# Weight sums kept in DRAM, and the sums of the seventh group's third block moved, in a routing-attention and squared-ReLU kernel

## The chip, the cores and the metric

The kernel runs on one core of a Trainium2 chip. The metric is the device time of one execution in microseconds (us). The median of three runs stands for a kernel, and a profiled execution of its own shows where the time goes. The page and the traces name the engines: PE is TensorE (PEld its weight loads), DVE is VectorE, ACT is ScalarE, POOL is GpSimd, and SP is SyncE, which here issues most of the DMAs.

## The reference, cut to what matters

```python
batch, n_heads, seq, head_dim = (4, 8, 768, 64); n_clusters = 16
n_tokens, d_model, d_ff = (3072, 512, 2048)
# attention, per batch and head: queries see only keys of their own cluster
mask = q_assign[:, :, :, None] == k_assign[:, :, None, :]
scores = np.where(mask, scale * q @ k.T, -1e9)
attn_out = softmax(scores) @ v
# its rows are the tokens of the second part
x = attn_out.transpose(0, 2, 1, 3).reshape(3072, 512)
h = x @ w_in                 # "up":   512 -> 2048
g = np.maximum(h, 0.0) ** 2
out = g @ w_out              # "down": 2048 -> 512
```

## The kernel before, in words

The attention comes first: 16 pairs of heads (`for p in range(NG)`), up to about 319 us. After it each of the four batches (`for n, b in enumerate(FEED)`) runs an up product with the squared ReLU into `g`, and a down product from `g` into the output. All instructions around the change are put out by hand, in program order on each engine (`manual_schedule`). Each engine, and SP with its DMAs, works through its own list in that order, and an instruction that waits holds up what is behind it on its list.

**Products by Strassen's scheme.** Both products save multiplications: a 2 x 2 block product is made by seven block products of sums of blocks. For the up product the sums of the weights are made by `w_sums(i)` for a group `i` of 0 to 7 (`F2` is 8): four operations on POOL fill one tile `w_s` of 128 x 1024 numbers (512 KB). There are two such tiles (tags `s1` and `s2`), used in turn. `w_sums` is called 8 times in every batch with the same weights, so 32 times. In batch 0 its first two calls stand at the ends of the last two attention pairs, and the others in `first_up`, one at the end of each group. In batches 1 to 3 the calls stand in `up`, one group ahead of use. In the down product the same two tags hold the second-level sums of a unit (`l`).

**Batch 0.** `first_up` runs eight groups. Each makes seven products into PSUM (`banks`: six buffers); ScalarE copies product 1 (L756), and VectorE adds the others into `g` (L750) in the order 6, 2, 7, 5, 4, 3 (`combine`). Between these additions `Rounding` brings the rest of the weights to their rounded form. It works on blocks of 512 columns: blocks 0 to 15 are `w_in`, 16 to 31 are `w_out`. A block is loaded by SP (L122, `load_ahead`), goes through two operations of ScalarE (L133, L139), three of VectorE (L145, L149, L153) and one of POOL (L161). `prepare(i)` stands behind the copy of group `i`: at `i = 0` it holds blocks 16 to 20, all on ScalarE and ahead of the copy of group 1. `behind` adds up the last pair's sums (L494) behind group 0. `first_down` is the down product of batch 0.

**Batches 1 to 3.** `up` runs the eight groups; a part of the products (all groups but the last two) has a second level of sums, whose weight sums also come from POOL (L839). When a group's results are squared, VectorE makes two kinds of sums of it for the down product: `first_level(g, f)` for the first two of the three column blocks, and `third_sums(g, n, f)` for the third block. The latter are four operations into a tile `third`, which a DMA stores in `g_far` (L1109); the blocks of `g` that are wanted as they are go there by `store_third` (L1096). For group 6 `third_sums` stands at the end of `up`, and its store is put out later by `Down.run` on ScalarE's queue; for group 7 it stands in `Down.run` behind the first unit.

`Down.run` goes through *units*, 14 in batches 1 and 3 and 7 in batch 2. A unit is seven products of four matmuls each (L1113), 6.26 us of TensorE. `parts` makes the sums of the next unit; `x[0][1] - s[:, 1]` (L1282, in the traces the helper's line L551) makes the operand of a unit's last product; `load_right` (L1072) brings the right-hand operands of the next unit, and `load_left` (L1151) those of the third block. `stage.parts` is passed to `up` as `behind_seven`, so that the first unit's sums are made inside `up`.

The traces give operations of small helpers the line of the helper: `sub` is L551, `plus` is L990, `matmul` of the up product L793.

Of the kernel before, what the change touches and what calls it, by code (L numbers as in the profile page):

```python
# [8 lines left out]
F32 = mybir.dt.float32  # L9
# [9 lines left out]
P = 128  # L19
# [6 lines left out]
def kernel(  # L26
# [10 lines left out]
    nc = tc.nc  # L37

    B, H, S, D = q.shape
# [19 lines left out]
    sp = ctx.enter_context(tc.tile_pool(name="sp", bufs=1))  # L59
    dram = ctx.enter_context(tc.tile_pool(name="dram", bufs=3, space=bass.MemoryType.DRAM))  # L60
    dram_x = ctx.enter_context(tc.tile_pool(name="dram_x", bufs=1, space=bass.MemoryType.DRAM))
# [135 lines left out]
    odd = const.tile([P, 2], F32, name="odd")  # L197
# [350 lines left out]
    H2, F2, M2 = KT // 2, FT // 2, DM // 2  # L548

    def sub(out, a, b, eng=nc.vector):  # L550
        return eng.tensor_tensor(out=out, in0=a, in1=b, op=ALU.subtract)  # L551
# [11 lines left out]
        sub(t4, t2, x[1][0])  # L563
        yield x, t1, t2, x[0][1], t4

    def w_sums(i, odd=0):
        lo, hi = slice(i * P, (i + 1) * P), slice((F2 + i) * P, (F2 + i + 1) * P)
        a = [[w_in[:, H2 * g2 : H2 * (g2 + 1), cols] for g2 in range(2)] for cols in (lo, hi)]
        w_s = sp.tile([P, 4, H2, P], F32, name="w_s", tag=f"s{(i + odd) % 2 + 1}")
        s1, s2, s3, s4 = (w_s[:, j] for j in range(4))  # L570
        nc.gpsimd.tensor_tensor(out=s1, in0=a[1][0], in1=a[1][1], op=ALU.add)  # L571
        sub(s2, s1, a[0][0], nc.gpsimd)
        sub(s3, a[0][0], a[1][0], nc.gpsimd)
        sub(s4, a[0][1], s2, nc.gpsimd)
        return a, s1, s2, s3, s4

    def tile_of(pair, i):
# [148 lines left out]
    def bank_tile(width):  # L726
        return banks.tile([P, width], F32, name="bank", tag="bank")
# [159 lines left out]
        plus(middle, c34, middle)  # L887
        yield

    def up(b, g, n, x, behind_seven, stores):  # L890
        flat = g.rearrange("p f h n -> p (f h n)")
        odd = n == B - 1
        w_next = w_sums(0, odd)
        lefts, rights, done = {}, {}, []
        for i in range(F2):
            w, w_next = w_next, w_sums(i + 1, odd) if i + 1 < F2 else None
            ((c11, c12), (c21, c22)), product = group(i, g, w, x)
            ends, late = i >= F2 - 2, i % 2

            def result(j):  # L900
                bank = bank_tile(TB)
                product(j, bank)
                return bank

            def add(j, *results):
                bank = result(j)
                for out, to in results:
                    plus(out, bank, to)

            def levels_1():  # L910
                if done:
                    first_level(g, done[0])

            def levels_2():
                if done:
                    third_sums(g, n, done.pop(0))()

            def two():
                add(2, (c11, c11))
                square(c11)  # L920
                if i < F2 - 1:
                    levels_2()

            if i < 2:
                nc.scalar.copy(out=c11, in_=result(1))
            elif not late:
                next(unit_1)
                if ends:
                    load_right(1)
            if not (late or ends):  # L930
                lefts[4] = second_lefts(4, i)
            add(6, (c12, c11))
            if i < F2 - 1:
                levels_1()
            if i == 1:
                rights[1] = second_rights(1, x[0][0][0])
            if not late or ends:
                two()
            if i == 0:
                rights[4] = second_rights(4, x[4])  # L940
            add(7, (c21, c12))
            if ends:
                levels_1()
            if i == F2 - 1:
                behind_seven()
            r = spare_tile.rearrange("p i n -> p (i n)")
            if late and not ends:
                unit_4 = second(lefts.pop(4), rights[4], r, 0, TB)
                next(unit_4)
            add(5, (c22, c21), (c12, c12))  # L950
            square(c22)
            if i == F2 - 2:
                levels_2()
            if ends:
                sub(c21, c21, result(4))
            elif late:
                next(unit_4)
                unit_1 = second(
                    second_lefts(1, i + 1), rights[1], flat, 2 * TB * (i + 1), 2 * TB
                )  # L960
                next(unit_1)
                both = g[:, F2 + i - 1 : F2 + i + 1, 0]
                sub(both, both, r.rearrange("p (i n) -> p i n", i=2))
                for k in range(2):
                    square(both[:, k])
                two()
            add(3, (c12, c12))
            if ends:
                square(c21)
            (square if i < F2 - 1 else square_by_dve)(c12)  # L970
            if i == F2 - 1:
                stores.append(third_sums(g, n, i - 1))
            done.extend([i] if ends else [i - 1, i] if late else [])
        xT.pop(b)

# [13 lines left out]
    def plus(out, one, two):  # L989
        nc.vector.tensor_tensor(out=out, in0=one, in1=two, op=ALU.add)  # L990
# [50 lines left out]
    g_far = [dram_x.tile([F2, P, 7, P], F32, name=f"g_far{n}") for n in range(B)]  # L1041
# [53 lines left out]
    def store_third(g, n, f, queue=nc.sync):  # L1095
        queue.dma_start(g_far[n][f, :, 1:3], g[:, F2 + f, :, THIRD])  # L1096
        if n % 2 == 0:
            queue.dma_start(g_far[n][f, :, 0], g[:, f, 0, THIRD])

    def third_sums(g, n, f):  # L1100
        if f < F2 - 1:
            store_third(g, n, f)
        a = block_of(g, f, THIRD)
        third = outp.tile([P, DM], F32, name="third", tag="osb").rearrange("p (j n) -> p j n", j=4)
        plus(third[:, 0], a[1][0], a[1][1])
        sub(third[:, 1], third[:, 0], a[0][0])
        sub(third[:, 2], a[0][0], a[1][0])
        sub(third[:, 3], a[0][1], third[:, 1])
        return lambda queue=nc.sync: queue.dma_start(g_far[n][f, :, 3:7], third)  # L1109

    def times(bank, left, rhs):
        for f in range(F4):
# [8 lines left out]

    class Down:
        def __init__(self, b, g, n):
            self.up_stores = []
            self.b, self.g, self.n = b, g, n
            both = n % 2
            self.units = (
                [(0, 1), (0, 4), (1, 4), (1, 1)] if both else [(0, 1), (0, 4)]
            ) + [(of, j) for j in RIGHT_ORDER[2:] for of in range(1 + both)]
            a = blocks(g, TWO)  # L1130
            s1, s2 = (s_home(i) for i in range(2))
            self.lefts = {
                1: a[0][0], 2: a[0][1], 3: s1, 4: a[1][1], 5: s1, 6: s2, 7: a[1][0]
            }
            self.a, self.s1, self.s2 = a, s1, s2
            self.count = 0
            self.stores = []
# [111 lines left out]
        def store(self, queue=nc.scalar):  # L1249
            for of, to in self.stores:  # L1250
                for i in range(2):
                    self.store_block(of, to, i, queue)
            self.stores = []

        def run(self):
            first_level(self.g, F2 - 1)
            waiting = None
            for u, (of, j) in enumerate(self.units):
                x, s = self.ahead
# [9 lines left out]
                times(one[:, 0], x[0][0], y[0][0])  # L1269
                nc.scalar.copy(out=copied, in_=one[:, 0])  # L1270
                if u == 0:
                    store_third(self.g, self.n, F2 - 1, nc.scalar)
                    self.up_stores.pop()(nc.scalar)
                self.store()
                times(two[:, 0], x[0][1], y[1][0])
                times(two[:, 1], s[:, 1], slot(1))
# [15 lines left out]
                        sub(self.s1, self.a[0][1], self.s2)  # L1292
                    self.parts()
                if u == 0:
                    store = third_sums(self.g, self.n, F2 - 1)
                    self.find_results()
                    if self.n % 2:
                        self.load_left(4)
                        self.load_left(1)
                    store()  # L1300
                if waiting:
                    next(waiting, None)
                waiting = self.combine(of, j, one, two, five, copied, last)
# [91 lines left out]
    x_summed = {}  # L1395
# [8 lines left out]
    for n, b in enumerate(FEED):  # L1404
        g = gp.tile([P, FT, 2, TB], F32, name="g")
        if n == 0:
            first_up(b, g, Rounding())
            first_down(b, g)
            again = nc.values_load(flag[0:1, 0:1], min_val=0, max_val=1)
            with tc.issue_after(last_w_sum[0]):  # L1410
                sum_x(1, 4)
            manual.enter_context(
                tc.manual_schedule(engines={E.PE, E.DVE, E.Activation, E.Pool, E.SP})
            )
            more = fast.enter_context(
                tc.tile_pool(name="more", bufs=2, space=PSUM, reuse_waits="tile")
            )
        else:
            stage = Down(b, g, n)
            up(b, g, n, x_summed.pop(n)[-1], stage.parts, stage.up_stores)  # L1420
            stage.run()
    manual.close()
    fast.close()
# [190 lines left out]
```

## Time and profile before

| what | value |
|---|---|
| median of 3 runs | 881.0 us (880.43 to 881.81) |
| the profiled execution | 880.63 us, of which span 878.8 us |
| TensorE busy | 870.7 us, granted clock 0.999 |
| VectorE busy | 755.9 us |
| ScalarE busy | 385.9 us |
| POOL busy | 182.4 us |
| DMA | 136.05 MB, mean 155 GB/s |

The stages of the span, from the trace:

| stage | us | TensorE busy | VectorE busy | POOL busy |
|---|---|---|---|---|
| attention | 0 to 319.4 | 317.8 | 274.0 | 24.7 |
| batch 0, up | 319.4 to 393.1 | 73.7 | 70.2 | 47.7 |
| batch 0, down | 393.1 to 441.8 | 48.7 | 43.6 | 3.2 |
| batch 1, up | 441.8 to 512.2 | 70.4 | 59.4 | 30.8 |
| batch 1, down | 512.2 to 599.8 | 87.6 | 71.7 | 5.4 |
| batch 2, up | 599.8 to 670.2 | 70.4 | 61.7 | 31.8 |
| batch 2, down | 670.2 to 714.1 | 43.9 | 38.8 | 5.3 |
| batch 3, up | 714.1 to 784.4 | 70.3 | 64.1 | 33.6 |
| batch 3, down, and the end | 784.4 to 878.8 | 87.9 | 72.3 | 0.0 |

How to read it: the span goes from the first instruction to the last, and the time of the execution is a little longer. TensorE's busy time counts a matmul from its start to a modelled end; consecutive matmuls overlap, so a mean duration in the page (0.486 us for 128 x 384) is longer than the distance at which such matmuls follow each other (9.03 us for 28 of them, so 0.3225 us). An f32 product of one tile shows as two matmul records. A wait is listed with the engine that ended it. In a timeline a line gives the start, the length, the engine, the line of the program, the operation with its output and inputs, how many instructions are merged, and in brackets the idle time ahead of it and what ended it.

### The profile page before, as it was taken

How to read it: one execution, taken by the hardware profiler on the slowest of the kernel's cores; microseconds unless marked ns; L12 is line 12 of the kernel's file. 1: busy time of each engine (PE TensorE's matmuls, PEld its weight loads, DVE VectorE, ACT ScalarE, POOL GpSimd, SP SyncE). 2: the span in 40 equal slices, each digit the busy share in tenths (PEclk: the TensorE clock that was granted, in tenths of full speed). 3: DMA queues.
4: the chain of work that ended last, by engine and by line, in shares of the span. 5: the costliest groups of instructions: out<-in, count | busy, mean ns of one | idle time of the engine just before them, and what ended most of it. 6: DMA issues, size and time to landing. Idle time of an engine off the chain costs nothing.

```text
span 878.8 us, 14998 instructions
## 1 busy us (share of the span) xinstructions
PE 870.7 (99%) x5487; PEld 597.9 (68%) x5487; DVE 755.9 (86%) x1359; ACT 385.9 (44%) x621; POOL 182.4 (21%) x240
## 2 busy tenths in 40 slices
PE   9999999999999999999999999999999999999997
PEld 5444444444444455568866689997767977769997
DVE  6799888888888999999859986797899898997786
ACT  5877667777765657750034420002543015440000
POOL 0000010000000236740055300005540064500000
PEclk9999999999999999999999999999999999999999
DMA  7777786866764235226701347681024730147563
GB/s 253 175 188 202 214 267 177 209 181 194 203 168 124 83 139 172 89 95 227 277 25 43 101 145 217 186 258 37 31 91 148 240 116 25 37 134 230 166 203 124
DMA packets 166402, 136.05 MB, mean 155 GB/s; under 512 B 58826, under 2 KB 140082, under 8 KB 166066
## 3 DMA queue, kind: packets, MB, share of 16 engines
q1 hardware_dynamic: 148546, 118.67, 45.7%
q10 hardware_dynamic: 17776, 16.36, 5.9%
q8 instruction: 45, 0.74, 0.3%
q14 instruction: 35, 0.29, 0.1%
HBM read 82.10 MB, written 41.89 MB: 141 GB/s over the span
## 4 chain that ended last, share of the span: by engine, by line
PE 98%; DVE 0%; DMA 0%; ACT 0%; issue 0%; DVEq 0%
PE bank L793 28%; PE bank L1113 25%; PE sc L441 14%; PE av_a L475 10%; PE bank L1005 6%; PE av_b L475 5%; PE sc L450 4%; PE bank L883 3%; PE sc L329 1%; PE more L883 1%; PE sc L494 1%; PE more L873 1%; DMA q_raw<-in_q_dram 0%; PE av_a L289 0%; ACT ex L457 0%; PE av_a L274 0%
## 5 line engine op out<-in xcount | busy, mean ns | idle before, releaser
L457 ACT ACTIVATE ex<-sc 128x1024 f32<-128x1024 f32 x144 | 144.4, 1026 | 37.5 <-PE sc L441 31.6
L441 PE MATMUL sc<-qkT 64*128 64x512 f32 (+1 forms) x768 | 150.5, 484 | 0.0
L990 DVE TENSOR_TENSOR g<-bank,g 128x384 f32<-128x384 f32 (+3 forms) x205 | 102.2, 515 | 21.1 <-PE bank L793 12.5
L769 ACT ACTIVATE g<-g 128x384 f32<-128x384 f32 x122 | 63.0, 516 | 96.5 <-DVE g L990 75.2
L441 PEld LDWEIGHTS sc<-qkT 64*128 64x128 f32 x768 | 65.6, 188 | 42.1 <-issue 30.2
L793 PE MATMUL bank<-xT,w_s 128*128 128x384 f32 x256 | 93.1, 486 | 0.0
L793 PE MATMUL bank<-x_t,w_s 128*128 128x384 f32 x256 | 93.0, 486 | 0.0
L1270 ACT COPY spare<-bank 128x128 f32<-128x128 f32 x35 | 9.3, 264 | 187.9 <-PE bank L1113 149.7
L475 PE MATMUL av_a<-ex,v_raw 128*64 128x512 f32 x384 | 85.9, 596 | 0.0
L460 DVE TENSOR_TENSOR total<-total,ex 128x1024 f32<-128x1024 f32 x64 | 78.7, 1229 | 6.5
L161 POOL TENSOR_TENSOR w_in<-w_in,w_raw 128x512 int32<-128x512 int32 x16 | 21.5, 1341 | 294.4 <-DVE w_in L153 294.4
L571 POOL TENSOR_TENSOR w_s<-w_in 128x256 f32<-128x256 f32 x32 | 26.3, 821 | 247.4 <-PE bank L1113 146.5
L1113 PE MATMUL bank<-home,l 128*128 128x128 f32 x560 | 74.0, 275 | 0.0
L793 PEld LDWEIGHTS bank<-xT,w_s 128*128 128x128 f32 x256 | 48.6, 190 | 34.3 <-issue 0.6
L1113 PEld LDWEIGHTS bank<-home,l 128*128 128x128 f32 x560 | 68.2, 192 | 0.0
L793 PEld LDWEIGHTS bank<-x_t,w_s 128*128 128x128 f32 x256 | 48.1, 190 | 29.1
L793 PE MATMUL bank<-xT,w_in 128*128 128x384 f32 x184 | 67.1, 487 | 0.0
L770 ACT ACTIVATE g<-g 128x384 f32<-128x384 f32 x122 | 63.8, 523 | 3.9
L475 PEld LDWEIGHTS av_a<-ex,v_raw 128*64 128x64 f32 x384 | 26.1, 137 | 51.0 <-issue 49.7
L450 PE MATMUL sc<-rows 64*128 64x512 bf16 (+1 forms) x360 | 58.8, 323 | 0.0
L793 PEld LDWEIGHTS bank<-xT,w_in 128*128 128x128 f32 x184 | 34.4, 190 | 21.7 <-DVE g L551 0.6
L1113 PE MATMUL bank<-home,g 128*128 128x128 f32 x352 | 46.5, 275 | 0.0
(221 smaller groups left out, 1560.6 us busy)
## 6 DMA issues: line engine op xcount, KB each, us to landing
home<-w_far SPq DMA_DIRECT2D x92, 256.0 KB
words<-flat SPq DMA_DIRECT2D x26, 384.0 KB
w_raw<-in_moe_w_in_dram SPq DMA_DIRECT2D x16, 512.0 KB
w_raw<-in_moe_w_out_dram SPq DMA_DIRECT2D x16, 512.0 KB
w_far<-home SPq DMA_DIRECT2D x28, 256.0 KB
g<-g_far SPq DMA_DIRECT2D x28, 256.0 KB
v_raw<-in_v_dram SPq DMA_DIRECT2D x16, 384.0 KB
rb<-far_r SPq DMA_DIRECT2D x30, 192.0 KB
```

The source lines that it names most:

```text
L441: nc.tensor.matmul(sc[i][:, e, cols], lhsT=qkT[pair][rows, NCH + c], rhs=qkT[pair][rows, n.start // P : n.stop // P], start=first, stop=no ...
L450: nc.tensor.matmul(sc[i][:, e, cols], lhsT=ohT[pair][rows, 1, c * P : (c + 1) * P], rhs=ohT[pair][rows, 0, columns(i)], start=first, stop= ...
L457: nc.scalar.activation(out=ex[i], in_=sc.pop(i), func=ACT.Exp, scale=SCALE)
L460: eng.tensor_tensor(out=out, in0=a, in1=b, op=ALU.add)
L475: nc.tensor.matmul(bank[D * e : D * (e + 1), 0 : n.stop - n.start], lhsT=raw_v[pair][:, e, c], rhs=ex[i][:, e, cols], start=c == 0, stop=c ...
L769: nc.scalar.activation(out=to, in_=to, func=ACT.Relu)
L770: nc.scalar.square(to, to)
L793: nc.tensor.matmul(bank, lhsT=operands[j][0][:, kk], rhs=operands[j][1][:, kk], start=(kk == 0), stop=(kk == H2 - 1),)
L883: nc.tensor.matmul(bank, lhsT=left, rhs=right, start=True, stop=True)
L990: nc.vector.tensor_tensor(out=out, in0=one, in1=two, op=ALU.add)
L1005: nc.tensor.matmul(bank, lhsT=left[j][:, f], rhs=right(j)[:, f], start=(f == 0), stop=(f == F2 - 1),)
L1113: nc.tensor.matmul(bank, lhsT=left[:, f], rhs=rhs[:, f], start=(f == 0), stop=(f == F4 - 1))
```

## The change

In batch 0 each `w_s` tile is also stored in DRAM, in a new tensor `sums_far` (8 x 512 KB). In batches 1 to 3 `w_sums` makes no sums: it issues a load of the tile from `sums_far`. Both DMAs stand on SP's list, at the place of the call. The argument `n` is the batch; the choice of the tag stays as it was. The three other parts of the diff belong together: `third_sums` of group 6 moves from the end of `up` into `Down.run`, beside that of group 7, which stands behind the `parts` of the second unit. Its `g` blocks are stored on ScalarE's queue with those of group 7, and both `third` tiles on SP behind the first left loads.

```diff
-    def w_sums(i, odd=0):
+    sums_far = dram_x.tile([F2, P, 4 * H2 * P], F32, name="sums_far")
+
+    def w_sums(i, n=0):
...
-        w_s = sp.tile([P, 4, H2, P], F32, name="w_s", tag=f"s{(i + odd) % 2 + 1}")
+        w_s = sp.tile([P, 4, H2, P], F32, name="w_s", tag=f"s{(i + n // (B - 1)) % 2 + 1}")
         s1, s2, s3, s4 = (w_s[:, j] for j in range(4))
+        flat = w_s.rearrange("p j k n -> p (j k n)")
+        if n:
+            nc.sync.dma_start(flat, sums_far[i])
+            return a, s1, s2, s3, s4
         nc.gpsimd.tensor_tensor(out=s1, in0=a[1][0], in1=a[1][1], op=ALU.add)
         sub(s2, s1, a[0][0], nc.gpsimd)
         sub(s3, a[0][0], a[1][0], nc.gpsimd)
         sub(s4, a[0][1], s2, nc.gpsimd)
+        nc.sync.dma_start(sums_far[i], flat)
         return a, s1, s2, s3, s4
...
-    def up(b, g, n, x, behind_seven, stores):
+    def up(b, g, n, x, behind_seven):
...
-        odd = n == B - 1
-        w_next = w_sums(0, odd)
+        w_next = w_sums(0, n)
...
-            w, w_next = w_next, w_sums(i + 1, odd) if i + 1 < F2 else None
+            w, w_next = w_next, w_sums(i + 1, n) if i + 1 < F2 else None
...
-            if i == F2 - 1:
-                stores.append(third_sums(g, n, i - 1))
...
     def third_sums(g, n, f):
-        if f < F2 - 1:
+        if f < F2 - 2:
             store_third(g, n, f)
...
                 if u == 0:
-                    store_third(self.g, self.n, F2 - 1, nc.scalar)
-                    self.up_stores.pop()(nc.scalar)
+                    for f in (F2 - 2, F2 - 1):
+                        store_third(self.g, self.n, f, nc.scalar)
...
                 if u == 0:
-                    store = third_sums(self.g, self.n, F2 - 1)
+                    stores = [third_sums(self.g, self.n, f) for f in (F2 - 2, F2 - 1)]
                     self.find_results()
                     if self.n % 2:
                         self.load_left(4)
                         self.load_left(1)
-                    store()
+                    for store in stores:
+                        store()
```

More of the change, by code (lines that the diff above doesn't have):

```diff
@@ L1108, in third_sums @@
         sub(third[:, 3], a[0][1], third[:, 1])
-        return lambda queue=nc.sync: queue.dma_start(g_far[n][f, :, 3:7], third)
+        return lambda: nc.sync.dma_start(g_far[n][f, :, 3:7], third)
     def times(bank, left, rhs):
@@ L1123, in __init__ @@
         def __init__(self, b, g, n):
-            self.up_stores = []
             self.b, self.g, self.n = b, g, n
@@ L1419 @@
             stage = Down(b, g, n)
-            up(b, g, n, x_summed.pop(n)[-1], stage.parts, stage.up_stores)
+            up(b, g, n, x_summed.pop(n)[-1], stage.parts)
             stage.run()
```

## The prediction

> **What bounds the kernel now.** I read the page first: TensorE is busy for nearly the whole span.
>
> ```profile
> PE 870.7 (99%) x5487; PEld 597.9 (68%) x5487; DVE 755.9 (86%) x1359; ACT 385.9 (44%) x621; POOL 182.4 (21%) x240
> ```
>
> Then the waits of TensorE alone. Outside the start of the program there is one; this is the whole list:
>
> ```profile
> PE bank L1113 <- DVE g L551: 1.4, 1, 1.4
> PE sc L179 <- DVE zeros L176: 1.1, 1, 1.1
> PE av_a L274 <- DMA q_raw<-in_q_dram: 0.5, 1, 0.5
> ```
>
> The first lies at the start of the last batch's down product. The timeline of VectorE there shows it without a gap: `third` (sums of block 6, four operations), then the first-level sums of block 7 (`home`, `home`, `g`), then the subtraction that TensorE waits for, which starts at 790.52.
>
> ```profile
> 788.27 0.28 DVE L990 TENSOR_TENSOR third<-g 128x128 f32<-128x128 f32 x1
> 788.59 0.29 DVE L551 TENSOR_TENSOR third<-third,g 128x128 f32<-128x128 f32 x1
> ...
> 789.20 0.42 DVE L990 TENSOR_TENSOR home<-g 128x256 f32<-128x256 f32 x1
> ...
> 790.52 0.69 DVE L551 TENSOR_TENSOR g<-g,l 128x512 f32<-128x512 f32 x1
> ```
>
> A table of stages finds a second tight place, the first up product (319.4 to 393.1): VectorE works 70.2 of 73.7 us there. Its groups follow each other by the first addition behind ScalarE's copy (L756 to L750). In the timeline these start at 341.65, 351.54, 361.45 and 371.36, so 9.90 us apart, while TensorE's 28 matmul records of a group take 28 x 0.3225 = 9.03 us. VectorE thus falls behind by 0.87 us a group and lives on the six banks. At 378.76 they are used up: a product that should follow 1.29 us behind 377.30 comes 0.17 us late.
>
> ```profile
> 377.30 1.45 PE L793 MATMUL bank<-xT,w_in 128*128 128x384 f32 x4
> 378.76 1.53 PE L793 MATMUL bank<-xT,w_s 128*128 128x384 f32 x4
> ```
>
> From there on a delay of VectorE is a delay of TensorE. What starts that chain is ScalarE, in order: it rounds blocks 17 to 20 of w_out as their loads land (the last three with an idle time that DMA ends), and only then copies the second group's first product at 331.06.
>
> ```profile
> 324.45 0.68 ACT L133 ACTIVATE w_out<-w_raw 128x512 f32<-128x512 f32 x1 [1.82 <-DMA w_raw<-in_moe_w_out_dram]
> 325.02 0.66 ACT L139 ACTIVATE low<-w_raw 128x512 f32<-128x512 uint32 x1
> 325.73 0.69 ACT L133 ACTIVATE w_out<-w_raw 128x512 f32<-128x512 f32 x1
> 327.69 0.68 ACT L133 ACTIVATE w_out<-w_raw 128x512 f32<-128x512 f32 x1 [1.27 <-DMA w_raw<-in_moe_w_out_dram]
> 328.95 0.70 ACT L133 ACTIVATE w_out<-w_raw 128x512 f32<-128x512 f32 x1 [0.59 <-DMA w_raw<-in_moe_w_out_dram]
> 329.55 1.37 ACT L139 ACTIVATE low<-w_raw 128x512 f32<-128x512 uint32 x2
> 331.06 0.48 ACT L756 COPY g<-bank 128x384 f32<-128x384 f32 x1
> ```
>
> Those four loads leave SP together at 320.85; the last operation of the second `w_s` on POOL ends at 325.05:
>
> ```profile
> 320.85 1.76 SPq L122 DMA_DIRECT2D w_raw<-in_moe_w_out_dram  x4
> ```
> ```profile
> 324.14 0.91 POOL L551 TENSOR_TENSOR w_s<-w_in,w_s 128x256 f32<-128x256 f32 x1
> ```
>
> **What the Trainium skill says.** "Perfetto Trace Analysis", The 4-stage abstract model: an instruction waits for its semaphores before it executes; with "DMA: Bandwidth & Descriptors", Anatomy of one DMA (DMA engines do not wait on semaphores, the issuing sequencer does), a waiting DMA therefore holds up all that is behind it on SP. The trace agrees: SP issues nothing between 305.98 and 320.85, though three of the four loads wait for other buffers than the first. "SBUF — State Buffer", Who interferes with whom: a VectorE operation with two SBUF inputs and a GpSimd operation that reads SBUF exclude each other for a whole instruction. The trace agrees: `third` operations take 0.28 us alone and 0.78 to 0.81 while POOL makes `w_s` (768.64 to 770.88).
>
> **The change part by part.**
>
> 1. *POOL's sums leave batches 1 to 3.* 24 of the 32 calls go: 24 x 4 operations of about 0.85 us = 82 us of POOL. POOL is on no chain, so by itself this is nothing. It frees VectorE: in the last batch three `third` operations behind 768.64 lose about 0.5 us each, 1.6 us in all, and as much after 749.9 in the group before. In batches 1 and 2 VectorE reaches the same subtraction at 516.67 and 674.68, 0.26 us ahead of need, after having even idled 0.36 us; relative to the stage's start the last batch is 1.6 us later. So the wait of 1.39 us goes by this part alone.
>
> 2. *Block 6's sums move behind the second unit's.* Four operations, 788.27 to 789.20, so 0.93 us, leave the place ahead of the subtraction in each of three batches. In batches 1 and 2 no wait is there to be saved; in the last they add 0.93 us of reserve. The work comes back behind `parts` of the second unit; the next subtraction, which now ends at 521.94 in batch 1, is needed at 512.26 + 6.26 + 5.36 = 523.88, so the 1.9 us cover it. On ScalarE's queue block 6's `third` store gives way to its `g` stores (one, in batch 2 two), 0.35 us each, with ScalarE idle 4.8 us behind; on SP one more `third` store comes behind the two left loads. Nothing. **Parts 1 and 2: -1.4 us**; from 0 to -1.6 (that wait and the 0.17).
>
> 3. *24 loads of 512 KB on SP.* No such row exists before. The nearest is a `w_raw` load of the same size: 3.6 us from issue (320.85) to use (324.45). The next `w_s` buffer is free when POOL now starts to fill it (L571: 449.67, 460.01, 468.41 and so on, 8.4 us or more apart) and is needed one such step later, so about 4.8 us of reserve. At the starts: batch 1, free 438.49, needed by the second product at 442.98, 0.9 us of reserve; batch 2, free 591.9, needed 601.2; batch 3, behind the last slot load (about 707.4), needed 715.4. Behind the waiting loads on SP stand `third` stores, whose data come later anyway, and the right-hand loads for the down product, needed 10 us later. I take nothing; bounds -0 and +2.6 us (a load of 7 us at batch 1).
>
> 4. *Eight stores of 512 KB on SP in batch 0.* Each waits for POOL. The first moves ahead of `far_r`, `rb` and block 16's load: SP goes on at 307.5 instead of 302.76. `rb` then lands about 312, needed at 315.68; block 16 is needed at 321.42. Nothing. The third to eighth stand behind loads that are already out, and the loads behind them wait for later POOL work anyway. **The second is the dear one**: the compiled order has block 16's load, this store, and then blocks 17 to 20. It waits until 325.05, so those leave at 325.5 to 326.8 instead of 320.85 to 322.6: +4.4 us. The store's own half megabyte goes ahead of theirs: the four landed about 1.5 us apart, so between 0 and 1.3 us more. Block 20 lands near 334.0 (333.3 to 334.7) instead of 328.95. ScalarE's copy follows it by 331.06 - 328.95 = 2.11 us: 336.1. VectorE's addition follows by 0.51: 336.6, against 332.42 before, where it had waited 0.5 us for TensorE. That is 4.2 us. One thing comes back: POOL makes the third `w_s` while VectorE waits and not beside its two rounding operations at 333.61 and 334.35 (0.71 and 0.83 instead of 0.43 each): -0.7. The chain starts 3.5 us late, has no idle time to recover in (0.2 us a group, and that is its own loop with ScalarE), and TensorE has no banks left at 378.76. **+3.5 us**, bounds 0 and +5.
>
> Sum: 3.5 - 1.4 = +2.1 us. The profiled execution took 880.63 us (span 878.8), 0.37 below the median of 881.0; so 882.7 for its like, and **883.1** as a median.
>
> **The rivals.**
>
> *The late blocks are hidden, and the change is a gain.* If block 20 lands by about 330, or the six banks carry more than I think, only part 1 and 2 count: 881.0 - 1.4 = 879.6. For it: TensorE waits in the trace by 0.17 us only in that whole stage. Against it: VectorE falls behind by 0.87 us a group, so these 0.17 are the end of its reserve. The sign turns where the first addition of the second group is 1.4 us late, at 333.8. All that TensorE loses from 319 us to its end is 73.7 - 224 x 0.3225 - 0.8 (the sums of L494) in the first up product and 1.4 later, some 2 us, so more than 0.2% of gain, 1.76 us (about what a measurement of this kernel can tell from no change), needs almost all of it.
>
> *The loads at the start of a batch are late.* If half a megabyte takes 7 us at 438.5, TensorE waits 2.6 us at 442.98, on top of part 4: 885.7. For it: only 0.9 us of reserve. Against: no other load is out then, and 3.6 us was measured with three more behind it.
>
> *The change doesn't do what it says.* The compiled order of the instructions shows POOL's operations gone and the loads in their place; I give this nothing.
>
> **How the numbers follow.** Forecast (late blocks, wait gone): 0.64, with 881.8 to 884.6 as its own range; of this 0.10 lies within 0.2%. Gain alone: 0.26, of which 0.10 is faster by over 0.2%, since 1.4 us is near the edge. Late loads besides: 0.10, slower. So faster 0.10, same 0.26, slower 0.64. The range goes from 879.5, which takes in most of the gain-only case, to 885.2.
>
> **What would show it.** Right: on SP a store of `sums_far` near 325.1 with four loads behind it; ScalarE's idle before L133 near 329 to 334 ended by DMA; its second copy near 336; the second group's first addition near 336.6; about 3.5 us of TensorE waits for VectorE, or of gaps between matmuls, before 390; no wait at the last down product, and `third` operations at 0.28 us. Wrong: the copy still near 331, or the first up product still 73.7 us long; a wait of L793's counterpart for `w_s<-sums_far`.

## The result, and the profile after

| | before | after |
|---|---|---|
| median | 880.57 us (879.86 to 881.81, 21 runs) | 882.33 us (880.95 to 884.2, 21 runs) |
| ratio after to before | | 1.002, 95% interval 1.0014 to 1.0026 |
| the profiled execution | 880.63 us, span 878.8 | 880.95 us, span 879.1 |
| batch 0, up | 73.67 us | 76.57 us |
| batch 3, down (to the last product) | 89.22 us | 87.56 us |
| the two other down products of batches 1 and 2 | | 0.12 us shorter together |

The change is slower, by 1.76 us in the medians. The profiled execution of after is the fastest of its 21 runs, so it explains the stages but not the whole difference of the medians. Its stages give +2.90 - 1.66 - 0.12 = +1.1 us; its attention ended 0.69 us earlier (318.83 against 319.52). In a second profile of the kernel before the attention also ended about 0.7 us earlier (first matmul of the up product at 318.79, not 319.45), so this is spread between executions and not the change.

The first line of the page: POOL lost 76 us of work and VectorE 15, while TensorE, which sets the time, is as busy as before.

```profile
PE 870.7 (99%) x5487; PEld 597.4 (68%) x5487; DVE 740.5 (84%) x1359; ACT 385.8 (44%) x621; POOL 106.1 (12%) x144
```

The waits of TensorE, the whole list (engine, line and what was waited for; total, times, longest). The wait of the last down product is gone; a new one stands in the first up product (L801, which was L793), on VectorE's additions (L758, which was L750):

```profile
PE bank L801 <- DVE g L758: 1.8, 3, 0.6
PE sc L179 <- DVE zeros L176: 1.1, 1, 1.1
PE av_a L274 <- DMA q_raw<-in_q_dram: 0.5, 1, 0.5
```

It can be followed back. SP's timeline: the second store (L582) leaves at 324.62, and the loads of blocks 17 to 20 only behind it (four of the six that are merged here).

```profile
324.62 0.33 SPq L582 DMA_DIRECT2D sums_far<-w_s  x1
325.05 4.15 SPq L122 DMA_DIRECT2D w_raw<-in_moe_w_out_dram  x6
```

ScalarE's timeline: idle for 7.41 us until block 17 lands, block 20 at 333.29, the copy of the second group's first product (L764) at 334.99.

```profile
329.36 0.66 ACT L133 ACTIVATE w_out<-w_raw 128x512 f32<-128x512 f32 x1 [7.41 <-DMA w_raw<-in_moe_w_out_dram]
...
333.29 0.68 ACT L133 ACTIVATE w_out<-w_raw 128x512 f32<-128x512 f32 x1 [0.63 <-DMA w_raw<-in_moe_w_out_dram]
333.88 1.18 ACT L139 ACTIVATE low<-w_raw 128x512 f32<-128x512 uint32 x2
334.99 0.47 ACT L764 COPY g<-bank 128x384 f32<-128x384 f32 x1
```

VectorE's timeline: the first addition of the second group at 335.49, behind 2.50 us without work. Put to a common clock (from the start of the stage) it comes 16.66 us in, against 12.90 before. The idle time is booked to a TensorE product; what came last was ScalarE's copy at 334.99.

```profile
335.49 0.56 DVE L758 TENSOR_TENSOR g<-bank,g 128x384 f32<-128x384 f32 x1 [2.50 <-PE bank L801]
...
336.70 0.46 DVE L149 TENSOR_SCALAR w_raw<-w_out 128x512 f32<-128x512 f32 x1
337.19 0.43 DVE L153 TENSOR_SCALAR w_out<-w_raw 128x512 uint32<-128x512 uint32 x1
```

The last down product in the chain of waits is one piece, where before it was broken between 787.21 and 791.27:

```profile
786.61 87.56 PE bank L1118 x784
```

### The profile page after: what moved, and what is told of

Same layout as the page of the kernel before. It is cut to its first block, busy times and chain, and to the rows that moved or that the text cites. A ratio compares the mean times of both kernels' runs of the same rounds, so it can differ in the third digit from the quotient of the medians.

```text
span 879.1 us, 14958 instructions
## 1 busy us (share of the span) xinstructions
PE 870.7 (99%) x5487; PEld 597.4 (68%) x5487; DVE 740.5 (84%) x1359; ACT 385.8 (44%) x621; POOL 106.1 (12%) x144
## 4 chain that ended last, share of the span: by engine, by line
PE 97%; DVE 1%; DMA 0%; ACT 0%; issue 0%
PE bank L801 26%; PE bank L1118 25%; PE sc L441 14%; PE av_a L475 10%; PE bank L1010 6%; PE av_b L475 5%; PE sc L450 4%; PE bank L891 3%; PE sc L329 1%; PE more L891 1%; PE sc L494 1%; DVE g L758 1%; PE more L881 1%; DVE w_raw L149 0%; DMA q_raw<-in_q_dram 0%; PE av_a L289 0%
## 5 line engine op out<-in xcount | busy, mean ns | idle before, releaser
L801 PE MATMUL bank<-xT,w_s 128*128 128x384 f32 x256 | 93.4, 488 | 1.9 <-DVE g L758 1.8
L801 PE MATMUL bank<-x_t,w_s 128*128 128x384 f32 x256 | 93.1, 486 | 0.0
L801 PEld LDWEIGHTS bank<-xT,w_s 128*128 128x128 f32 x256 | 48.4, 190 | 37.0 <-issue 4.2
L801 PEld LDWEIGHTS bank<-x_t,w_s 128*128 128x128 f32 x256 | 48.3, 190 | 29.0
L801 PE MATMUL bank<-xT,w_in 128*128 128x384 f32 x184 | 67.1, 487 | 0.0
L847 POOL TENSOR_TENSOR home<-w_in 128x128 f32<-128x128 f32 x18 | 9.0, 499 | 343.8 <-PE bank L891 129.4
L801 PEld LDWEIGHTS bank<-xT,w_in 128*128 128x128 f32 x184 | 34.5, 190 | 21.7 <-DVE g L551 0.6
```

Of the source, the lines that this page charges most:

```text
L801: nc.tensor.matmul(bank, lhsT=operands[j][0][:, kk], rhs=operands[j][1][:, kk], start=(kk == 0), stop=(kk == H2 - 1),)
```

## The experiments

### The place of the second store

**Second store behind the four loads.** Everything else as in after.

```diff
+        def store():
+            nc.sync.dma_start(sums_far[i], flat)
+        if i == 1:
+            late_stores.append(store)
+        else:
+            store()
...
# behind the loads of blocks 17 to 20
+    late_stores.pop()()
```

> The changed kernel, but the store of the second w_s tile is put out behind the loads of blocks 17 to 20 on SP, not ahead of them; all bytes stay. Order theory (the four loads are late because a store that waits for POOL stands ahead of them): the first up product is back at 73.7 us (76.6 in the changed kernel's profile), the loads leave near 320.9, and the 1.4 to 1.8 us gained in the last batch remain: 880.6 - 1.6 = 879.0 us. Bytes theory (4 MB of stores slow the loads wherever they stand): first up product 75 us or more, 881 to 882 us. Later-loads theory (the loss lies in the loads of batches 1 to 3): no change against the changed kernel, 882.3 us.

Measured: 879.26 us, ratio to before 0.9986 (0.9976 to 0.9995). The first up product takes 73.58 us, as before, and the wait for VectorE is gone. TensorE's waits, the whole list, and SP's timeline of this kernel:

```profile
PE sc L179 <- DVE zeros L176: 1.1, 1, 1.1
PE av_a L274 <- DMA q_raw<-in_q_dram: 0.4, 1, 0.4
```

```profile
320.36 1.76 SPq L122 DMA_DIRECT2D w_raw<-in_moe_w_out_dram  x4
324.58 0.33 SPq L584 DMA_DIRECT2D sums_far<-w_s  x1
```

The place of one of the 32 added DMAs costs 3.0 us (1.0020 - 0.9986 = 0.34%). The next three kernels ask what it is about that place: the wait of SP ahead of the loads, or the half megabyte that goes ahead of theirs.

**A small store at the old place.** As the last kernel, and at the old place one number of each partition, so 128 pieces of 4 bytes.

```diff
+            nc.sync.dma_start(sums_near, w_s[:, 3, 1, P - 1 : P])
```

> store_late with one small store added: at the place where the change has the store of the second w_s, 128 numbers (one of each partition, 512 bytes) of that tile go to DRAM; the full store stands behind the four loads. So SP waits for POOL there as in the changed kernel, but no half megabyte goes ahead of the loads. Order theory, split: if the wait alone makes the loss, block 20 lands at about 333 as in the changed kernel (333.29) and the time is 879.3 + 3.0 = 882.3 us. If the bytes ahead of the loads make a third of it (1.3 us of landing), block 20 lands 1.3 us earlier and the time is 881.0 us. Bytes theory: 879.3 us, as store_late.

Measured: 889.2 us, ratio 1.0093 (1.0078 to 1.0109), far beyond both expectations. ScalarE's timeline and the waits of TensorE:

```profile
337.52 0.66 ACT L133 ACTIVATE w_out<-w_raw 128x512 f32<-128x512 f32 x1 [14.35 <-DMA w_raw<-in_moe_w_out_dram]
```
```profile
PE bank L810 <- ACT g L773: 6.9, 1, 6.9
```

The loads leave SP at 326.45, but block 17 lands 11.1 us later instead of some 4, and between 328 and 336 the DMA moves 0 to 53 GB/s (in windows of 2 us), against 377 to 418 in after between 328 and 334. So the small pieces held up the loads behind them, and this run says nothing on the question that it was made for.

**The small store again, as one piece.** 512 contiguous bytes of one partition.

```diff
+            nc.sync.dma_start(sums_near, w_s[0:1, 3, 1, :])
```

> As store_late (the second store of the sums behind the four loads), with one more store at the old place: 128 numbers of the second w_s from one partition, 512 contiguous bytes, which wait for POOL's last operation like the full store but move almost nothing. Order theory (the loads cost time because they stand behind a waiting store on SP): loads leave near 325.5, the first up product again near 76.5 us, 882.2. Bytes theory (the half megabyte ahead of theirs counts): as store_late, 879.3. Half each would be near 880.8.

Measured: 881.68 us, ratio 1.0013 (1.0004 to 1.0021); the first up product takes 76.49 us. SP's timeline, and the waits of TensorE:

```profile
324.49 0.26 SPq L588 DMA_DIRECT2D sums_near<-w_s  x1
324.85 1.77 SPq L122 DMA_DIRECT2D w_raw<-in_moe_w_out_dram  x4
```
```profile
PE bank L810 <- DVE g L767: 1.9, 3, 0.6
```

ScalarE's timeline:

```profile
328.45 0.68 ACT L133 ACTIVATE w_out<-w_raw 128x512 f32<-128x512 f32 x1 [6.55 <-DMA w_raw<-in_moe_w_out_dram]
...
333.29 0.67 ACT L133 ACTIVATE w_out<-w_raw 128x512 f32<-128x512 f32 x1 [0.94 <-DMA w_raw<-in_moe_w_out_dram]
...
334.98 0.48 ACT L773 COPY g<-bank 128x384 f32<-128x384 f32 x1
```

Half a kilobyte does most of what half a megabyte did. The order, a waiting store ahead of ready loads, is thus the main cause: it makes 2.4 of the 3.0 us (1.0013 - 0.9986 = 0.27%). The other 0.6 us would be the bytes, but the intervals of the two kernels (1.0004 to 1.0021, and 1.0014 to 1.0026 for after) overlap. That block 20 lands at 333.29 in both profiles doesn't settle it: the profile of after is its fastest, and here the full store went out right behind the loads, at 326.66. The other profiles say more. From the issue of the first of the four loads to the first operation on block 17 it is 4.31, 4.88 and 5.04 us in the three profiles with the half megabyte directly ahead (after twice, and the stores alone, below), and 3.51 to 3.70 in nine without it. To block 20 it is 8.24 to 8.93 us against 7.50 to 8.44. So the bytes do delay the loads a little, block 17 by 0.6 us or more; at block 20, on which the copy waits, the ranges overlap.

**The same bytes without the wait.** At the old place, the first `w_s` once more (512 KB), whose data were ready; the second store late.

```diff
+            nc.sync.dma_start(sums_near, made.pop())   # the first w_s again
```

> As store_late, with one more store of 512 KB at the old place, of the first w_s once more, whose data were ready long ago: the same bytes ahead of the four loads and no wait. Order theory: loads leave near 320.9, each block lands 0 to 1.3 us later than in store_late, block 20 by 330.2; that is inside the reserve of 1.4 us, so 879.3 to 880.0. Bytes theory: the first up product near 76.5 us, 882.2.

Measured: 878.9 us, ratio 0.9977 (0.997 to 0.9985); the first up product takes 73.53 us. SP's timeline:

```profile
311.44 0.43 SPq L589 DMA_DIRECT2D sums_near<-w_s  x1
320.08 1.76 SPq L122 DMA_DIRECT2D w_raw<-in_moe_w_out_dram  x4
```

This store went out 8.6 us before the loads, not beside them, so that it shows less than meant: half a megabyte more on SP is free there. What bytes directly ahead of the loads cost, it does not show.

### The parts of the change

**The stores alone.** The kernel before plus the eight stores; POOL makes the sums of all batches, and nothing moves.

```diff
+        if n == 0:
+            nc.sync.dma_start(sums_far[i], flat)
```

> The kernel before with the eight stores of batch 0 added at the places of the change; POOL still makes the sums in all batches, and the third-block sums stay where they were. Order theory: +2.9 us in the first up product and the wait of 1.4 us in the last batch stays: 880.6 + 2.9 = 883.5 us. Bytes theory: the same. Later-loads theory: 880.6 us, no loss in the first up product.

Measured: 882.79 us, ratio 1.0027 (1.0015 to 1.0038). The waits of TensorE:

```profile
PE bank L799 <- DVE g L756: 1.9, 3, 0.6
...
PE bank L799 <- ACT g L762: 0.6, 1, 0.6
```

The loss is there as expected. But the wait of the last down product, which nothing here touches, is gone too; neither theory had that.

**The stores alone, the second one late.**

> stores_only with the second store behind the four loads; POOL makes all sums in all batches. Order theory: no loss in the first up product (73.7 us), so 880.8 us as the kernel before, or down to 879.3 us if the wait in the last batch is absent as it was in the profile of stores_only. Bytes theory: 882.8 us, as stores_only.

Measured: 879.3 us, ratio 0.9986 (0.9979 to 0.9992), the first up product 73.77 us, and again no wait in the last down product. But for the place of the second, no cost of the stores is seen, and the gain of 1.3 us comes without any load.

**Stores and loads, nothing moved** (the second store late).

> store_late without the move of the third-block sums: loads instead of POOL in batches 1 to 3, the second store behind the four loads. Theory by the shared port (POOL's sums slowed VectorE by 1.6 us or more in the last batch): the wait of 1.39 us goes without the move, so 879.0 us, as store_late. Rival (the move is what removes it): a wait of about 1.4 us stays in the last batch, 880.6 us.

Measured: 879.06 us, ratio 0.9985 (0.9977 to 0.9993). No wait, all `third` operations of the last batch take 0.28 us.

**The move alone.** POOL makes all sums, no DMA is added.

> The kernel before with only the move of the third-block sums of group 6 (no stores, no loads; POOL makes all sums). Theory by VectorE's backlog: the four operations (0.93 us) leave the place ahead of the subtraction, so the wait of 1.39 us falls to about 0.46 us: 880.6 - 0.9 = 879.7 us. Rival (the moved work meets the next unit and the wait only comes one unit later): 880.6 us, with a wait at the second unit's last product.

Measured: 878.91 us, ratio 0.9982 (0.9974 to 0.999). No wait either; 0.93 us of it had been expected to go, and some 0.5 to stay. The move is not the only thing that differs here, as the next section shows.

**Both kernels profiled again.**

> The kernel before, profiled once more. stores_only and thirds_only showed no wait in the last batch though POOL makes the sums there and, in stores_only, nothing was moved. If that wait depends on how VectorE's and POOL's operations happen to meet, it can be absent here, and the time is then about 879.3 us; if it is always there, it shows 1.39 us again and the time is about 880.7 us.

> The changed kernel, profiled once more. The first up product should again be near 76.6 us and the last batch without a wait. If the landing of blocks 17 to 20 varies (block 20 at 333.3 in the first profile; in stores_only 1.4 us later), the product's length varies with it, 76 to 78 us, and so does the time, 881 to 883 us.

Measured: 880.05 us for before, with the same wait of 1.4 us; 882.84 for after, with the second store at 325.88, block 20 at 335.05, and the first up product 76.75 us long. In this one block 17 landed 4.88 us behind the issue of its load instead of 4.31, and besides, TensorE lost 1.3 us to a late transfer in the attention. Such differences can make the spread of after.

### Who comes first, POOL or VectorE

Every kernel so far except before had lost the wait of the last down product. The timelines of before and of the stores alone with the second one late, laid over each other from the start of batch 3's up product, agree up to 30.2 us. There VectorE goes on at once in the second and idles 0.46 us in before. First before, then the stores alone with the second one late:

```profile
745.32 1.02 DVE L990 TENSOR_TENSOR g<-bank,g 128x384 f32<-128x384 f32 x2 [0.46 <-PE bank L883]
```
```profile
744.43 1.67 DVE L1001 TENSOR_TENSOR g<-bank,g 128x384 f32<-128x384 f32 x3
```

At the four `third` operations, at 35.8 us, POOL starts its `w_s` 0.18 us before VectorE in the one kernel, and 0.18 us behind it in the other. Where POOL is first, every `third` operation is slow; where VectorE is first, only two are. In the stores alone and in the move alone VectorE is first as well. The latter's first lines of VectorE and POOL at the last of these collisions:

```profile
766.44 0.28 DVE L988 TENSOR_TENSOR third<-g 128x128 f32<-128x128 f32 x1
```
```profile
766.62 0.73 POOL L571 TENSOR_TENSOR w_s<-w_in 128x256 f32<-128x256 f32 x1 [1.74 <-PE bank L793]
```

So the kernel with the move alone had lost the slow order too, and what the move itself would save is not separated from that.

**A later POOL.** The kernel before with one small operation more on POOL, in the last batch only.

```diff
+        if odd:
+            nc.gpsimd.tensor_tensor(out=s1[:, 0], in0=a[1][0][:, 0], in1=a[1][1][:, 0], op=ALU.add)
         nc.gpsimd.tensor_tensor(out=s1, in0=a[1][0], in1=a[1][1], op=ALU.add)
```

> The kernel before, with one small POOL operation more (a part of s1, written over at once by the whole) ahead of each set of sums in the last batch: POOL starts w_s about 0.4 us later there, nothing else changes. Collision theory (who of POOL and VectorE comes first at the third operations, 0.18 us apart, decides over 1.4 us): VectorE comes first, two of four third operations take 0.28 us again, the wait at the last down product goes or falls under 0.5 us: 879.4 with an interval below 1. Rival (the wait goes in the other kernels for another reason): 880.7 to 881.5, with the wait of 1.4 us still there.

Measured: 878.89 us, ratio 0.9978 (0.997 to 0.9987): more work, and 2.0 us less time. TensorE has no wait in the last down product. VectorE's and POOL's timelines at the last of these collisions, first of the kernel before:

```profile
768.25 0.35 DVE L990 TENSOR_TENSOR third<-g 128x128 f32<-128x128 f32 x1
768.64 0.78 DVE L551 TENSOR_TENSOR third<-third,g 128x128 f32<-128x128 f32 x1
769.34 0.81 DVE L551 TENSOR_TENSOR third<-g 128x128 f32<-128x128 f32 x1
770.07 0.81 DVE L551 TENSOR_TENSOR third<-g,third 128x128 f32<-128x128 f32 x1
```
```profile
768.54 0.73 POOL L551 TENSOR_TENSOR w_s<-w_s,w_in 128x256 f32<-128x256 f32 x1
```

and of the kernel with the later POOL:

```profile
767.74 0.28 DVE L992 TENSOR_TENSOR third<-g 128x128 f32<-128x128 f32 x1
768.05 0.74 DVE L551 TENSOR_TENSOR third<-third,g 128x128 f32<-128x128 f32 x1
768.72 0.28 DVE L551 TENSOR_TENSOR third<-g 128x128 f32<-128x128 f32 x1
768.92 0.81 DVE L551 TENSOR_TENSOR third<-g,third 128x128 f32<-128x128 f32 x1
```
```profile
767.92 0.73 POOL L573 TENSOR_TENSOR w_s<-w_in 128x256 f32<-128x256 f32 x1
```

Before, the second `third` operation starts 0.10 us behind a POOL operation, and from there each one runs up against the next of POOL's: 2.75 us for the four, against 2.11. The same happens at 749.89, two groups earlier. A later POOL with nothing else changed takes the wait away, so the wait hung on the order of the two engines. What makes VectorE 0.35 us later in before than in the kernel with the stores alone and the second one late is the idle 0.46 us shown above. It is no lateness of TensorE: the first of the L883 matmuls that the profile names starts 30.68 us behind the batch's first matmul in both kernels (744.62 and 744.74). The same idle time stands in the second profile of before and in the kernel with the later POOL, and not in the stores alone or the move alone. Why one addition waits in some kernels and not in others, with the same code in batch 3, stays open. With the later POOL, VectorE comes to the first collision even later (36.3 us behind the batch's first matmul, against 35.95 in before) and TensorE still doesn't wait. The gain of 2.0 us has an interval from 1.1 to 2.6, in which the wait of 1.4 lies.

## Why the prediction was right, point by point

The forecast, slower with the late blocks outweighing the wait that goes, is what happened, and by the mechanism named: 1.76 us against a forecast of 2.1.

**Part 4, the second store.** Forecast 3.5 us, measured 2.9 in the stage (76.57 - 73.67), and 3.0 by moving that store alone. From the start of the stage (319.52 and 318.83), block 20 was to land 14.48 us in and landed 14.46 in; in the second profile of after it was 14.7, so the agreement to 0.02 is luck. The term that was mis-sized is the step from block 20 to the copy: 2.11 us were carried over from before, and it took 1.70. Before, the two L139 operations ahead of the copy took 1.37 us together, now 1.18. In five of the eight profiles with early loads there is an idle time between these two that VectorE's L145 ended (0.24 to 0.67 us); in after it is not there, which fits a VectorE that had no other work then. The addition thus came 3.76 us late rather than 4.2, and 0.65 came back at L149 and L153 (0.46 and 0.43 instead of 0.71 and 0.83), for which 0.7 was put in. The rest, 3.1, reached TensorE almost whole (2.9): the six banks were no reserve, as argued. The half megabyte of the store itself was given 0 to 1.3 us; the landing of block 20 behind the issue of the loads, 8.24 to 8.93 us against 8.10 in the profile of before, puts it at 0.1 to 0.8 us. What the skill says in "Perfetto Trace Analysis", The 4-stage abstract model, a wait ahead of execution, accounts for most of it on SP: the 512-byte store shows the wait alone costing 2.4 of the 3.0 us.

**The other stores.** Forecast nothing; the stores alone with the second late took 879.3 us, which is before without its wait of 1.4 us.

**Part 3, the loads.** Forecast nothing, with 0.9 us of reserve at the start of batch 1. No wait for `w_s<-sums_far` is in the list. The first load of batch 1 left at 440.64, and the first product that reads it ran at 445.2, 4.5 us later, without a wait; so the load took no longer than that. How much shorter it was isn't to be seen.

**Parts 1 and 2.** Forecast -1.4, from 0 to -1.6; measured -1.66 - 0.12 in the three down products, and 1.2 to 2.0 us by the ratios of the kernels that gain without the loss. The size held, a little beyond the range; the reasoning behind it held only in part. "This part alone" removes the wait, true, and the way there, VectorE's slow `third` operations beside POOL, is the right one. But part 2 alone was to give at most 0.93 and the kernel with it lost the whole wait, and neither part is needed: 0.5 us of lateness on POOL is enough. The step that failed is the reading of the wait as the cost of POOL's work. It was the cost of an unlucky order of two engines. It went with loads in POOL's place, but also in the kernels with the move alone, with the stores alone and with a later POOL, all of which keep POOL's work. In batches 1 and 2 nothing was to be saved, and 0.12 us was; it comes with the move (87.54 and 43.77 us for the two down products in the move alone, 87.60 and 43.83 before). POOL's saving itself was put at 82 us and was 76, which changed nothing.

**The rivals.** The gain without the loss (879.6 forecast) is what after becomes with one store moved: 879.26. Its place of turn, an addition 1.4 us late, was passed by 2.4 us. Late loads at the start of a batch did not happen.

**A better version.** After with the second store behind the loads beats both kernels (0.9986 of before), but the move of block 6's sums alone does as well (0.9982), and so does the small POOL operation (0.9978); their intervals overlap. What they gain, 1.2 to 1.9 us, is in the main the wait that before had by the order of two engines; that before had this wait to lose is an accident of order, and the change looks 1.4 us better for it. The 76 us of POOL's work bought nothing that can be seen: the kernel with loads in place of the sums (0.9985) and the one in which POOL makes them all (0.9986) take the same time.

## What to carry to other kernels

When a DMA is added to an in-order queue, ask what it waits for and which transfers stand behind it; here the place of one waiting store cost 3.0 us, 2.4 of it with a store of half a kilobyte in its place. A wait of one or two microseconds at one place of one batch, where like batches have none, may come of the order in which two engines reach a shared resource; shift one of them by half a microsecond before building anything to remove it. Test each part of a change alone, and look in its trace for what else has moved: here two parts and an unrelated half microsecond all took the same 1.4 us away.

## What the runs showed of the hardware that was not expected

- **128 pieces of 4 bytes held up the transfers behind them for some 7 us.** With that store the first load took 11.1 us from issue to use (326.45 to 337.52), with one piece of 512 bytes 3.6 us (324.85 to 328.45). "DMA: Bandwidth & Descriptors", Specifications, names 512 bytes as the smallest size for the full rate and says that below it the engine reads, changes and writes back. The run agrees in direction; whether that is the mechanism no run shows.
- **A store directly ahead delays the loads behind it, a little.** With 512 KB going out just before them the first of four loads took 4.31 to 5.04 us from issue to use (three profiles), without it 3.51 to 3.70 (nine). By the fourth load the ranges overlap.
- **A few tenths in the order of two engines can grow.** Four operations of VectorE took 2.11 us where it started first and 2.75 where POOL did. Between before and the stores alone with the second one late VectorE's start differed by 0.35 us at the first collision (35.95 and 35.60 us behind the batch's first matmul) and by 1.6 at the last `third` sums of `up` (74.33 and 72.73); 1.4 of that became a wait of TensorE. "SBUF — State Buffer", Who interferes with whom, states that the order of issue decides who blocks; the kernel with the later POOL agrees. That a block lasts for a whole instruction is said there in so many words only of VectorE's two-port modes; here a `third` operation took 0.78 to 0.81 us instead of 0.28 beside POOL operations of 0.73 to 0.77.
